# Two linear-attention and feed-forward layers on one core: banks by age, statistics from accumulating ops, a reordered attention phase

## The chip, the cores and the metric

The kernel runs on one core of a Trainium2 chip. The metric is device time in microseconds of one execution; a run's time is given as the median of several. The engines are PE (TensorE), DVE (VectorE), ACT (ScalarE), POOL (GpSimd) and SP (SyncE, which here only issues DMAs).

## The reference, cut to what matters

```python
def _A_ref(x, wqkv, wo):             # H = 32 heads of 16, D = 512, S = 2048
    q, k, v = qkv[0], qkv[1], qkv[2]
    phi = lambda t: jnp.where(t > 0, t + 1, jnp.exp(t)) + 1e-6
    pq, pk = phi(q), phi(k)
    kv = jnp.einsum("bhsd,bhse->bhde", pk, v)
    z = jnp.einsum("bhsd->bhd", pk)
    num = jnp.einsum("bhqd,bhde->bhqe", pq, kv)
    den = jnp.einsum("bhqd,bhd->bhq", pq, z)[..., None] + 1e-6
    return (num / den).transpose(...).reshape(B, S, D) @ wo
def _B_ref(x, w_gate, w_up, w_down):  # F = 1792
    return (_silu(x @ w_gate) * (x @ w_up)) @ w_down
x = x + _A_ref(_layernorm(x), A_wqkv, A_wo)
x = x + _B_ref(_layernorm(x), B_w_gate, B_w_up, B_w_down)
x = x + _A_ref(_layernorm(x), A_wqkv, A_wo)
x = x + _B_ref(_layernorm(x), B_w_gate, B_w_up, B_w_down)
```

## The kernel before

All weights and the activations X stay in SBUF. The 2048 tokens are 16 tiles of 128, or four groups of 512 (four tiles each). Layers are numbered 0 to 3: 0 and 2 are attention, 1 and 3 feed-forward.

**Layer norm** (`ln`, L402). For one tile, DVE takes statistics (L408, L409), POOL makes variance plus epsilon and its power -0.5 (L410, L413), and ACT applies them (L426, after one more POOL operation, L422) or, for the first four tiles, DVE (L430). The normalised tile is then transposed into xnT: by a DMA transpose that SP issues (L445), or, for the first four tiles, by PE with a copy by DVE (L438, L442).

**Attention.** `k_proj` makes a tile's k in four matmuls; `phi` (L452) turns it into pk by an exponential on ACT (L454), a minimum on DVE (L456) and a DVE operation that reads the bank again (L459). `g_acc` accumulates G = xn^T pk over all 16 tiles in banks 0 to 3, `z_acc` the sum of pk. `g_copy`, `kvt`, `m_mm` make from G the matrix Mo that takes the place of v, kv and wo. `q_proj` makes a chunk (128 features) of a group's q, with phi. `den` (L536) multiplies q by z in 16 small matmuls, takes the reciprocal on DVE, spreads it on ACT (L553), has it transposed by four DMAs from SP (L557) and multiplies it into the four chunks of q on DVE (L562), each over the whole group. `wo` (L566) multiplies a tile by Mo, adds into X on DVE (L573) and starts the next layer's `ln`.

**Feed-forward.** `gu` makes one of 14 chunks of gate and up for a group, with a tanh on ACT and two DVE operations; `dn` multiplies a tile by w_down, adds into X (L611) and starts the next `ln`.

**Order.** PE's order is the order in which the code calls these functions, written out by hand (L660 to L720); `weave` mixes a list of fill blocks into a feed-forward group. The other queues are ordered by `schedule` (L58): it places each instruction by costs given in the code (`occ`, `lat`), takes what can start earliest on an engine, and breaks ties by a due time worked back from PE's order. Every queue then runs in that fixed order on the chip and waits on semaphores. X's seven loads (L372 to L379) are such ties; their `lat` is 2.3 for tile 0, 3.0 + 0.5t for tiles 1 to 3. PSUM has eight banks: gate and up take 0 to 3 in turn, k and q banks 4 and 5, the rest 6 and 7. The weights are 15 DMAs from POOL of 256 to 512 KB: two at once, then one after each key tile of layer 0, at most four in flight.

In layer 0 the key phase runs k_proj of all 16 tiles with g_acc two tiles behind. Then come z, g_copy, kvt, m_mm, q of groups 0 to 2 with their den, and wo of groups 0 and 1; gate and up of layer 1 start, with the rest of q, den and wo as fill. In layer 2 the key tiles 0 to 11 are fill of layer 1's groups, and g_acc follows.

Of the kernel before, what the change touches and what calls it, by code (L numbers as in the profile page):

```python
# [11 lines left out]
SEM = 0.06  # L12


class Op:
    __slots__ = ("i", "eng", "fn", "deps", "occ", "lat", "dma", "lane", "start", "end", "need", "val",
                 "dead", "succ", "pos", "tag")


class Prog:  # L20
# [5 lines left out]
    def __init__(self, lanes):  # L26
        self.ops = []
        self.bufs = {}
        self.lanes = lanes

    def op(self, eng, fn, r=(), w=(), occ=0.5, lat=None, after=(), dma=False, tag=""):
        o = Op()
        o.i = len(self.ops)
        o.eng, o.fn, o.occ, o.dma, o.tag = eng, fn, occ, dma, tag
        o.lat = lat if lat is not None else occ + 0.09
        o.need = dma
# [18 lines left out]
        self.ops.append(o)  # L55
        return o

    def schedule(self):  # L58
# [4 lines left out]
        t = 0.0  # L63
        pe_time = {}
        for o in ops:
            if o.eng == "pe":
                pe_time[o.i] = t
                t += o.occ
        for o in reversed(ops):
            dead = t + 50.0  # L70
            for s in o.succ:
                s = ops[s]
                dead = min(dead, s.dead - o.lat - SEM)
            if o.eng == "pe":
                dead = min(dead, pe_time[o.i])
            o.dead = dead
        nd = {o.i: len(o.deps) for o in ops}
        free = {e: 0.0 for e in self.ENGINES}
# [4 lines left out]
        xbar = 0.0  # L83
# [21 lines left out]
        while left:  # L105
            best = None
            for e in self.ENGINES:
# [7 lines left out]
                cand = None  # L115
                for o in avail[e]:
                    s = max(free[e], rt_of[o.i])
                    key = (s, o.dead, o.i)
                    if cand is None or key < cand[0]:
                        cand = (key, o)  # L120
                if cand is not None and (best is None or cand[0][0] < best[0]):
                    best = (cand[0][0], cand[1])
# [4 lines left out]
            if o.dma == "t":  # L127
                xbar = max(xbar, s + 0.6) + 1.0
                o.end = xbar + 1.2
            else:  # L130
                o.end = s + o.lat
# [123 lines left out]
def bass_interleave_layers__linear_attn_block__swiglu_ffn__prompt_kernel(  # L255
# [20 lines left out]
    with stack:  # L276
# [9 lines left out]
        negh = sb("negh", [P, 1], FP32)  # L286
        Wqkv = sb("Wqkv", [P, NC, 3 * D], BF16)
# [14 lines left out]
        nmr = sb("nmr", [P, T], FP32)  # L302
        NE = 4
        etmp = [sb("etmp", [P, 512], BF16) for _ in range(NE)]
        pk = [sb("pk", [P, D], BF16) for _ in range(T)]
        NPQ = 12
        pq = [sb("pq", [P, 512], BF16) for _ in range(NPQ)]
        GT = sb("GT", [P, NC, D], BF16)
        KVT = sb("KVT", [P, NC, P], BF16)
        Mo = sb("Mo", [P, NC, D], BF16)  # L310
# [13 lines left out]
        r_gu = Ring([0, 1, 2, 3])  # L324
        r_kq = Ring([4, 5])
        r_tok = Ring([6, 7])
# [9 lines left out]
        r_ost = Ring(range(8, NPQ))  # L336
# [13 lines left out]
        op("pool", lambda g: g.memset(negh[:], -0.5), w=["negh"], occ=0.1)  # L350
        op("pool", lambda g: g.memset(ident[:], 0.0), w=["ident"], occ=0.2)
# [4 lines left out]
        def late_consts(after):  # L356
            mask3 = mask[:].rearrange("p (h j) -> p h j", j=DH)
            op("pool", lambda g: g.memset(ones[:], 1.0), w=["ones"], occ=0.1, after=after)
# [276 lines left out]
        for t in range(TG, T):  # L635
            ln(0, t)
# [118 lines left out]
```

## Time and profile before

| | us |
|---|---|
| median of 3 runs | 476.61 (474.79 to 477.08) |
| the profiled execution, its own time | 478.77 |
| its span, first to last instruction | 477.0 |
| PE busy in the span | 435.2 (91%) |
| DVE busy | 327.8 (69%) |
| ACT busy | 171.6 (36%) |
| POOL busy | 77.2 (16%) |
| mean granted clock of PE | 0.964 of 2.4 GHz |

Busy shares are means over stages that differ, so the span has to be cut before they say anything. Matmul records overlap by design: 0.38 us of one matmul's record is not its cost, the start-to-start distance is.

### The profile page before, as it was taken

The page shows a single profiled execution, that of the slowest core. Times are in us where ns is not written, and L with a number is a line of the kernel's source. Part 1 is how long each engine was busy: PE and PEld are TensorE (multiplying, and loading weights), DVE is VectorE, ACT ScalarE, POOL GpSimd, SP SyncE. Part 2 cuts the span into 40 slices and gives each one's busy share as a digit, 9 for nine tenths or more (in the row PEclk, how much of TensorE's full clock was granted, in tenths as well). Part 3 has the DMA queues.
Part 4 walks back from the last instruction along what each step waited for, and adds up shares of the span by engine and source line. Part 5 has one row for each costly group of instructions (what it writes and reads, how often), then busy time and mean ns, then how long its engine had stood idle before and what let it go on. Part 6 is the DMA issues. An engine that isn't in the chain of part 4 may idle for free.

```text
span 477.0 us, 6447 instructions
## 1 busy us (share of the span) xinstructions
PE 435.2 (91%) x2182; PEld 194.2 (41%) x2182; DVE 327.8 (69%) x613; ACT 171.6 (36%) x277; POOL 77.2 (16%) x214
## 2 busy tenths in 40 slices
PE   4788967899999999999999996678999999999997
PEld 1333522244444444444444342223444444444443
DVE  3964679599679858867873267959856873763761
ACT  0672452645334414324322135263532331321320
POOL 3871103311122020012003000331100110000000
PEclk9799977799999999999999997999999999999999
DMA  8399522421221111001001002242221012001001
GB/s 276 82 230 159 202 56 45 88 43 37 44 45 23 24 22 23 0 9 38 0 1 34 11 2 56 45 80 48 41 45 43 12 22 57 1 2 44 1 0 44
DMA packets 56656, 24.27 MB, mean 51 GB/s; under 512 B 50672, under 2 KB 55280, under 8 KB 56624
## 3 DMA queue, kind: packets, MB, share of 16 engines
q1 hardware_dynamic: 54512, 16.27, 16.1%
q0 software_dynamic: 1584, 7.08, 5.6%
q10 hardware_dynamic: 528, 0.52, 0.4%
q8 instruction: 17, 0.28, 0.2%
q14 instruction: 15, 0.12, 0.1%
HBM read 9.70 MB, written 2.10 MB: 25 GB/s over the span
## 4 chain that ended last, share of the span: by engine, by line
PE 73%; DVE 9%; DMA 7%; SPq 5%; POOL 2%; issue 2%; ACT 2%; DVEq 0%; ACTq 0%; POOLq 0%
PE pb L343 72%; DMA xnT<-xnA 3%; SPq L557 3%; DMA RT<-rrep 2%; SPq L445 2%; DVE stats L408 2%; DVE pq L459 2%; DVE X L573 1%; DMA X<-in_A_x_dram 1%; POOL rstd L413 1%; DVE pq L562 1%; ACT etmp L454 1%; DVE etmp L456 1%; POOL vpe L410 1%; DVE Mo L500 1%
## 5 line engine op out<-in xcount | busy, mean ns | idle before, releaser
L343 PE MATMUL pb<-xnT,Wg 128*128 128x512 bf16 x448 | 115.8, 381 | 5.5 <-DMA xnT<-xnB 5.3
L343 PE MATMUL pb<-xnT,Wu 128*128 128x512 bf16 x448 | 115.9, 381 | 1.4 <-DVE hT L596 1.4
L591 ACT ACTIVATE tht<-pb 128x512 f32<-128x512 f32 x112 | 66.5, 595 | 124.5 <-PE pb L343 112.9
L343 PE MATMUL pb<-Wd,hT 128*128 128x512 bf16 x448 | 98.0, 379 | 0.0
L593 DVE SCALAR_TENSOR_TENSOR tht<-tht,pb 128x512 f32<-128x512 f32 x112 | 76.5, 683 | 26.3 <-ACT tht L591 25.7
L596 DVE TENSOR_TENSOR hT<-tht,pb 128x512 bf16<-128x512 f32 x112 | 76.8, 686 | 9.8 <-DVE mv L409 0.4
L343 PEld LDWEIGHTS pb<-xnT,Wg 128*128 128x128 bf16 x448 | 43.8, 98 | 59.6 <-issue 7.4
L343 PEld LDWEIGHTS pb<-xnT,Wu 128*128 128x128 bf16 x448 | 44.0, 98 | 55.2 <-DVE hT L596 2.1
L343 PEld LDWEIGHTS pb<-Wd,hT 128*128 128x128 bf16 x448 | 43.7, 98 | 52.4
L410 POOL TENSOR_SCALAR vpe<-mv 128x1 f32<-128x1 f32 x64 | 14.6, 236 | 288.6 <-DVE mv L409 287.4
L454 ACT ACTIVATE etmp<-pb 128x512 bf16<-128x512 f32 x64 | 37.9, 594 | 64.4 <-PE pb L343 57.5
L408 DVE BATCH_NORM_STATS2 stats<-X 128x6 f32<-128x512 bf16 x64 | 42.8, 682 | 7.4 <-DMA X<-in_A_x_dram 6.6
L456 DVE TENSOR_SCALAR etmp<-etmp 128x512 bf16<-128x512 bf16 x64 | 18.8, 294 | 36.0 <-ACT etmp L454 34.5
L343 PE MATMUL pb<-Mo,pq 128*128 128x512 bf16 x128 | 36.1, 419 | 6.0 <-DVE pq L562 4.5
L343 PE MATMUL pb<-xnT,Wqkv 128*128 128x512 bf16 x128 | 36.9, 421 | 4.9 <-DVE pq L459 3.4
L343 PE MATMUL pb<-Wqkv,xnT 128*128 128x512 bf16 x128 | 34.0, 390 | 5.6 <-DMA xnT<-xnA 2.1
L426 ACT ACTIVATE xnB<-X,nmr,rstd 128x512 bf16<-128x512 bf16 x32 | 25.3, 809 | 36.8 <-POOL nmr L422 30.6
L426 ACT ACTIVATE xnA<-X,nmr,rstd 128x512 bf16<-128x512 bf16 x28 | 22.7, 812 | 42.9 <-POOL nmr L422 42.9
L413 POOL TENSOR_TENSOR rstd<-vpe,negh 128x1 f32<-128x1 f32 x64 | 36.2, 570 | 5.5 <-POOL vpe L410 0.5
L343 PE MATMUL pb<-pk,xnA 128*128 128x512 bf16 x128 | 31.1, 379 | 0.0
L611 DVE SCALAR_TENSOR_TENSOR pq<-pb,X 128x512 bf16<-128x512 f32 x16 | 11.1, 691 | 28.9 <-PE pb L343 28.9
L459 DVE SCALAR_TENSOR_TENSOR pk<-pb,etmp 128x512 bf16<-128x512 f32 x32 | 22.1, 690 | 2.7
(51 smaller groups left out, 231.5 us busy)
## 6 DMA issues: line engine op xcount, KB each, us to landing
out_dram<-pq SPq DMA_DIRECT2D x16, 128.0 KB, 1.7
Wg<-in_B_w_gate_dram POOLq DMA_DIRECT2D x4, 448.0 KB, 7.5
Wu<-in_B_w_up_dram POOLq DMA_DIRECT2D x4, 448.0 KB, 10.7
X<-in_A_x_dram SPq DMA_DIRECT2D x3, 512.0 KB, 9.2
Wd<-in_B_w_down_dram POOLq DMA_DIRECT2D x3, 512.0 KB, 6.6
Wqkv<-in_A_wqkv_dram POOLq DMA_DIRECT2D x2, 512.0 KB, 6.8
Wqkv<-in_A_wqkv_dram ACTq DMA_DIRECT2D x1, 512.0 KB, 4.4
X<-in_A_x_dram SPq DMA_DIRECT2D x4, 128.0 KB, 4.4
```

The costliest lines, as they stand in the source:

```text
L343: return op("pe", lambda e: e.matmul(o_ap, lhsT=lhsT, rhs=rhs, start=start, stop=stop, skip_group_check=skip), r=r, w=w, occ=occ, lat=occ ...
L408: op("dve", lambda v: v.bn_stats(stats[:, t, :], X[:, t, :]), r=[xk], w=[f"st{t}"], occ=0.6)
L410: op("pool", lambda p: p.tensor_scalar(out=vpe[:, t:t + 1], in0=mv[:, t, 1:2], scalar1=1e-5, scalar2=None, op0=ALU.add), r=[f"mv{t}"], w=[ ...
L413: op("pool", lambda p: p.tensor_tensor(out=rstd[:, t:t + 1], in0=vpe[:, t:t + 1], in1=negh[:], op=ALU.pow), r=[f"vp{t}", "negh"], w=[f"rs{ ...
L426: op("act", lambda a: a.activation(out=b_ap, in_=X[:, t, :], func=ACT.Identity, bias=nmr[:, t:t + 1], scale=rstd[:, t:t + 1]), r=[xk, f"nm ...
L454: op("act", lambda a: a.activation(out=etmp[e][:], in_=PB[pb][:], func=ACT.Exp), r=[f"pb{pb}"], w=[f"e{e}"], occ=0.485, lat=0.6)
L456: op("dve", lambda v: v.tensor_scalar(out=etmp[e][:], in0=etmp[e][:], scalar1=1.0, scalar2=1e-6, op0=ALU.min, op1=ALU.add), r=[f"e{e}"], w ...
L459: op("dve", lambda v: v.scalar_tensor_tensor(out=dst, in0=PB[pb][:], scalar=0.0, in1=etmp[e][:], op0=ALU.max, op1=ALU.add), r=[f"pb{pb}", ...
L557: op("sp", lambda e, tl=tl, q=q: e.dma_start(RT[R][:, :, tl * P:(tl + 1) * P], rrep[q][:], transpose=True), r=[f"rrep{q}"], w=[f"RT{R}_{tl ...
L591: op("act", lambda e: e.activation(out=tht[a][:], in_=PB[pg][:], func=ACT.Tanh, scale=0.5), r=[f"pb{pg}"], w=[f"th{a}"], occ=0.485, lat=0.6)
L593: op("dve", lambda v: v.scalar_tensor_tensor(out=tht[a][:], in0=tht[a][:], scalar=1.0, in1=PB[pg][:], op0=ALU.add, op1=ALU.mult), r=[f"pb{ ...
L596: op("dve", lambda v: v.tensor_tensor(out=hT[h][:, j, :], in0=tht[a][:], in1=PB[pu][:], op=ALU.mult), r=[f"pb{pu}", f"th{a}"], w=[f"h{h}_{ ...
```

## The change

- **Planner.** Ties on a queue go by due time among all instructions that can start within 0.1 us (`HOLD`); DMAs are modelled by two pipes with a transfer time each; a DMA may carry a fixed priority. X's loads and the key weights get one, in tile order; the key weights are two DMAs instead of one, the larger X loads 256 KB instead of 512.
- **PSUM.** Banks are given by age: the one whose last use lies furthest back; the four banks of G and the one of z are pinned while they accumulate.
- **Layer norm.** In layers 1 to 3 the sum of X comes from the adding operation itself (`accum_out` in wo and dn), and the sum of squares from a Square on ACT; one small DVE operation makes the negative mean. The apply is on DVE, in layer 0 from tile 4 on wherever planned load is lighter. The first four tiles' transposes are copied out by ACT.
- **phi.** Two forms, chosen by planned load: as before, or with the add on ACT (a second activation from the bank) and a maximum on DVE from SBUF.
- **q and den.** A group's q is one tile, and the multiply by the reciprocal goes by token tile, each after its own transpose. Mo is written over G.
- **Order.** The key phase takes z along, and in layer 0 eight q products (groups 0 and 1). q of group 3 moves from the feed-forward fill ahead of it. The weights start after key tile 7, two per tile.

```diff
-            o.dead = dead
+            o.dead = dead if o.prio is None else o.prio
...
+                at = {o.i: max(free[e], rt_of[o.i]) for o in avail[e]}
+                lim = min(at.values()) + HOLD
+                o = min((o for o in avail[e] if at[o.i] <= lim), key=lambda o: (o.dead, o.i))
...
-        r_gu = Ring([0, 1, 2, 3])
-        r_kq = Ring([4, 5])
-        r_tok = Ring([6, 7])
+        def bank(pin=False):
+
+            def last(b):
+                st = pr.bufs.get(f"pb{b}")
+                return max([st[0]] + st[1] + [stamp[b]]) if st else stamp[b]
+            b = min((b for b in range(8) if b not in pinned), key=lambda b: (last(b), b))
...
+        for t in range(TG):
+            dma("sp", X[:, t, :], x2d[t * P:(t + 1) * P, :], 128, w=[f"x{t}"], prio=-100 + t)
+        dma("act", Wqkv[:, 0:2, D:2 * D], wq3[:, 0:2, D:2 * D], 256, w=["Wk0"], prio=-100)
+        dma("act", Wqkv[:, 2:4, D:2 * D], wq3[:, 2:4, D:2 * D], 256, w=["Wk1"], prio=-99)
...
+                op("dve", lambda v: v.tensor_scalar(out=mv[:, t, 0:1], in0=sums[:, t:t + 1], scalar1=-1.0 / D,
+                                                    scalar2=None, op0=ALU.mult),
+                   r=[f"sm{t}"], w=[f"mv{t}"], occ=0.07, lat=0.14)
+                op("act", lambda a: a.activation(out=b_ap, in_=X[:, t, :], func=ACT.Square,
+                                                 bias=mv[:, t, 0:1], accum_out=mv[:, t, 1:2]),
+                   r=[xk, f"mv{t}"], w=[bk, f"ss{t}"], occ=0.62, lat=0.75)
...
-                op("dve", lambda v: v.tensor_copy(out=dst, in_=tp[:, 0:512].rearrange("p (c k) -> p c k", c=NC)),
-                   r=[f"pb{pb}"], w=[f"xt{sl}_{tl}"], occ=0.4)
+                op("act", lambda a: a.activation(out=dst, in_=src, func=ACT.Copy),
+                   r=[f"pb{pb}"], w=[f"xt{sl}_{tl}"], occ=0.664, lat=0.77)
...
+            if mode == "act":
+                op("act", lambda a: a.activation(out=dst, in_=PB[pb][:], func=ACT.Identity, bias=onep[:]),
+                   r=[f"pb{pb}", "onep"], w=dk, occ=0.485, lat=0.6)
...
+            if mode == "act":
+                op("dve", lambda v: v.tensor_tensor(out=dst, in0=dst, in1=etmp[e][:], op=ALU.max),
+                   r=[f"e{e}"] + dk, w=dk, occ=0.335, lat=0.42)
...
+                op("dve", lambda v, ap=ap, tl=tl: v.tensor_tensor(out=ap, in0=ap,
+                                                                  in1=RT[R][:, :, tl * P:(tl + 1) * P], op=ALU.mult),
+                   r=ks + [f"RT{R}_{tl}"], w=ks, occ=0.335, lat=0.42)
...
-            op("dve", lambda v: v.tensor_tensor(out=X[:, t, :], in0=PB[pb][:], in1=X[:, t, :], op=ALU.add),
-               r=[f"pb{pb}", f"x{t}"], w=[f"x{t}"], occ=0.607, lat=0.69)
+            op("dve", lambda v: v.scalar_tensor_tensor(out=X[:, t, :], in0=PB[pb][:], scalar=1.0, in1=X[:, t, :],
+                                                       op0=ALU.mult, op1=ALU.add, accum_out=sums[:, t:t + 1]),
...
-        for i in range(14):
+        spin(11)
+        ln(0, 0, pe_t=True)
+        spin(2)
...
         for t in range(T):
+            if t < TG - 1:
+                ln(0, t + 1, pe_t=True)
             k_proj(0, t)
...
+            if t >= 7:
+                load_next(2)
             if t >= LAG:
-                g_acc(t - LAG)
+                gz(0, t - LAG)
+            if t >= 10:
+                q(0, *divmod(t - 10, NC))
+        q(0, 1, 2)
+        gz(0, T - 2)
+        q(0, 1, 3)
+        gz(0, T - 1)
...
         for L in (0, 2):
+            z_fin(L)
+            g_copy()
+            if L == 2:
+                q(L, 0, 2, 3)
+                q(L, 1, 0, 1, 2, 3)
+            else:
+                q(L, 2, 0)
+            den(L, 0)
             kvt()
+            q(L, 2, 1)
             m_mm()
+            q(L, 2, 2)
             den(L, 1)
+            q(L, 2, 3)
+            wos(L, 0)
+            q(L, 3, 0)
+            wos(L, 1, [0, 1])
+            q(L, 3, 1)
+            wos(L, 1, [2, 3])
+            q(L, 3, 2, 3)
             den(L, 2)
```

## Rows read from the trace of the kernel before

**Rows 1.** Stages: length, busy PE, PEld, DVE, ACT, POOL; clock, DMA share, GB/s.

```profile
15.30:52.00 36.70, 32.18 (x143) 13.05 (x142) 23.47 (x56) 19.73 (x32) 19.48 (x48) 0.97 0.83 186
52.00:89.30 37.30, 26.86 (x205) 11.72 (x202) 29.50 (x66) 16.98 (x30) 5.88 (x16) 0.82 0.28 65
89.30:257.50 168.20, 167.96 (x784) 75.93 (x785) 127.44 (x223) 64.98 (x102) 26.92 (x77) 0.99 0.14 27
257.50:279.60 22.10, 21.04 (x151) 9.85 (x150) 6.67 (x14) 5.26 (x9) 1.32 (x4) 1.00 0.09 17
279.60:316.00 36.40, 24.36 (x146) 10.01 (x145) 29.34 (x66) 17.42 (x31) 5.89 (x18) 0.86 0.23 45
316.00:477.00 161.00, 156.17 (x736) 70.52 (x736) 104.05 (x170) 46.35 (x76) 10.88 (x31) 1.00 0.13 30
```

**Rows 2.** Timeline, 0 to 61 us: start, duration, engine, line, operation, [idle before].

```profile
0.80 3.47 SPq L369 DMA_DIRECT2D X<-in_A_x_dram  x7
...
7.82 0.69 DVE L408 BATCH_NORM_STATS2 stats<-X 128x6 f32<-128x512 bf16 x1 [6.63 <-DMA X<-in_A_x_dram]
...
11.15 0.59 PE L438 MATMUL pb<-ident,xnA 128*128 128x128 bf16 x4 [5.27 <-POOL vpe L410]
...
14.44 1.28 ACT L426 ACT_TABLE_LOAD   x1 [14.44 <-POOL nmr L422]
...
15.29 3.17 PE L343 MATMUL pb<-Wqkv,xnT 128*128 128x512 bf16 x8
...
59.60 0.55 PE L343 MATMUL pb<-Zm,pq 128*128 128x8 bf16 x16
```

**Rows 3.** The chain that ended last, in order of time: start, duration, what.

```profile
2.18 5.62 DMA X<-in_A_x_dram
...
63.25 1.19 SPq L557
64.53 1.22 SPq L557
...
67.16 2.45 DMA RT<-rrep
...
138.41 130.54 PE pb L343 x604
```

**Rows 4.** Waits of PE: engine, line, releaser: us in total, times, longest.

```profile
PE pb L343 <- DVE pq L459: 10.7, 13, 2.6
PE pb L343 <- DMA xnT<-xnB: 5.3, 2, 3.0
```

**Rows 5.** DMA issues (first X load; POOL's Wqkv; transposes from 32 to 34 us): median us to landing.

```profile
X<-in_A_x_dram SPq DMA_DIRECT2D x1, 128.0 KB, 2.2
...
Wqkv<-in_A_wqkv_dram POOLq DMA_DIRECT2D x2, 512.0 KB, 6.8
...
xnT<-xnA SPq DMA_TRANSPOSE x2, 13.2
```

**Rows 6.** Groups by line and shape: busy us, mean ns | idle before it.

```profile
L408 DVE BATCH_NORM_STATS2 stats<-X 128x6 f32<-128x512 bf16 x64 | 42.8, 682 | 7.4 <-DMA X<-in_A_x_dram 6.6
...
L454 ACT ACTIVATE etmp<-pb 128x512 bf16<-128x512 f32 x64 | 37.9, 594 | 64.4 <-PE pb L343 57.5 <-DVE pk L459 4.5 <-DVE pq L459 1.1
...
L459 DVE SCALAR_TENSOR_TENSOR pk<-pb,etmp 128x512 bf16<-128x512 f32 x32 | 22.1, 690 | 2.7
...
L456 DVE TENSOR_SCALAR etmp<-etmp 128x512 bf16<-128x512 bf16 x64 | 18.8, 294 | 36.0 <-ACT etmp L454 34.5
...
L562 DVE TENSOR_TENSOR pq<-pq,RT 128x512 bf16<-128x512 bf16 x32 | 12.1, 418 | 5.8 <-DMA RT<-rrep 5.8
...
L409 DVE BATCH_NORM_AGGREGATE mv<-stats 128x2 f32<-128x6 f32 x64 | 10.0, 171 | 1.8
...
L430 DVE TENSOR_SCALAR xnA<-X,mv,rstd 128x512 bf16<-128x512 bf16 x4 | 1.6, 402 | 0.2 <-POOL rstd L413 0.2
```

**Rows 7.** Windows: the 17th microsecond, columns as in Rows 1.

```profile
16.00:17.00 1.00, 1.00 (x4) 0.30 (x3) 1.00 (x3) 0.55 (x1) 0.82 (x4) 0.50 0.00 0
```

More of the change, by code (lines that the diff above doesn't have):

```diff
@@ L29, in __init__, with lighter, after, op @@
         self.lanes = lanes
-    def op(self, eng, fn, r=(), w=(), occ=0.5, lat=None, after=(), dma=False, tag=""):
+        self.clock = {e: 0.0 for e in self.ENGINES}
+    def lighter(self, **loads):
+        def after(name):
+            c = dict(self.clock)
+            for e, x in loads[name].items():
+                c[e] = max(c[e], c["pe"]) + x
+            return max(c["act"], c["dve"]), sum(loads[name].values())
+        return min(loads, key=after)
+    def op(self, eng, fn, r=(), w=(), occ=0.5, lat=None, after=(), dma=0.0, prio=None):
         o = Op()
         o.i = len(self.ops)
-        o.eng, o.fn, o.occ, o.dma, o.tag = eng, fn, occ, dma, tag
+        o.eng, o.fn, o.occ, o.dma, o.prio = eng, fn, occ, dma, prio
         o.lat = lat if lat is not None else occ + 0.09
-        o.need = dma
+        o.need = dma > 0
         o.succ = []
@@ L55, in op @@
         self.ops.append(o)
+        c = self.clock
+        c[eng] = (c[eng] if eng == "pe" else max(c[eng], c["pe"])) + occ
         return o
@@ L62, in schedule @@
                 ops[d].succ.append(o.i)
[L63 to L68, printed above, removed]
+        t = sum(o.occ for o in ops if o.eng == "pe")
+        after = t
         for o in reversed(ops):
@@ L74, in schedule @@
             if o.eng == "pe":
-                dead = min(dead, pe_time[o.i])
-            o.dead = dead
+                dead = after = min(dead, after - o.occ)
+            o.dead = dead if o.prio is None else o.prio
         nd = {o.i: len(o.deps) for o in ops}
-        free = {e: 0.0 for e in self.ENGINES}
+        free = {e: 0.6 for e in self.ENGINES}
+        free["act"] = 0.61
         avail = {e: [] for e in self.ENGINES}
@@ L114, in schedule @@
                     continue
[L115 to L122, printed above, removed]
+                if not avail[e]:
+                    continue
+                at = {o.i: max(free[e], rt_of[o.i]) for o in avail[e]}
+                lim = min(at.values()) + HOLD
+                o = min((o for o in avail[e] if at[o.i] <= lim), key=lambda o: (o.dead, o.i))
+                if best is None or at[o.i] < best[0]:
+                    best = (at[o.i], o)
             assert best is not None, "stuck"
@@ L126, in schedule @@
             free[o.eng] = s + o.occ
-            if o.dma == "t":
-                xbar = max(xbar, s + 0.6) + 1.0
-                o.end = xbar + 1.2
+            if o.dma:
+                k = o.lat > 2.5
+                pipe[k] = max(pipe[k], s + o.occ + 0.9) + o.dma
+                o.end = pipe[k] + 0.6
             else:
@@ L480, in z_acc @@
             if L not in zb:
-                zb[L] = r_tok.take()
+                zb[L] = bank(pin=True)
             pb = zb[L]
@@ L504, in g_copy @@
             for c in range(NC):
-                evac(c, GT[:, c, :], f"GT{c}", "act" if c % 2 == 0 else "dve")
+                evac(gb[c], GT[:, c, :], f"GT{c}")
+                pinned.discard(gb[c])
         def kvt():
-            pb = r_tok.take()
+            pb = bank()
             for c in range(NC):
@@ L527, in q_proj @@
             sl = slot_of[L, g]
-            pb = r_kq.take()
+            pb = bank()
             for c in range(NC):
@@ L584, in gu @@
             sl = slot_of[L, g]
-            pg, pu = r_gu.take(), r_gu.take()
+            pg, pu = bank(), bank()
             for pb, W, wk in ((pg, Wg, "Wg"), (pu, Wu, "Wu")):
@@ L601, in dn @@
             h = hb[L, g]
-            pb = r_tok.take()
+            pb = bank()
             for j in range(NF):
```

270 lines of the change are left out of this document (136 added, 134 removed).

## The prediction

> **What bounds the kernel now.** I first cut the span into its stages at matmul landmarks [rows 1]: key phase of layer 0 (K1), its attention part (A1), its feed-forward part (B1), and the same for layer 2 (K2, A2, B2), with the start ahead of them. In B1 TensorE is busy 167.96 of 168.20 us and in B2 156.17 of 161.00, so nothing off TensorE is worth anything there. The loss sits in the start, where the first key matmul comes at 15.29 [rows 2], and in A1 and A2, where TensorE is busy 26.86 of 37.30 and 24.36 of 36.40 us. Its granted clock averages 0.82 and 0.86 of 2.4 GHz there, so part of the busy time is at the lower level, 1.2 GHz.
>
> To see how much of a stage is work I price a 512-column matmul at full clock: 604 of them in 130.54 us [rows 3], 0.216 us each, 0.86 for the four of a product. A1 holds 40 for q, 32 for wo and 4 for Mo: 16.4 us. Its 128 small ones (64 for z, 48 for den, 16 for KVT) go at 0.034, as 16 for den take 0.55 [rows 2]: 4.4. So 20.8 of 37.3 us is work and 16.5 is lost. A2 has no z to speak of: 18.6 is work and 17.8 lost.
>
> Next, which wait ends last: TensorE waits for phi's vector instruction to free a bank (10.7 us in 13 waits) and for transposes of the normalised tiles (5.3 us) [rows 4]. The chain shows where the latter come from [rows 3]: den, reciprocal, broadcast, then transposes that SyncE issues one by one, 1.28 us apart, the last landing 2.45 us after its issue ends. VectorE is busy 29.50 of A1's 37.30 us [rows 1].
>
> **Start.** The first statistic runs at 7.82 after a wait of 6.63 us, though the first 128 KB transfer, issued at 0.80, landed within 2.2 [rows 2, 5]. The fourth ended at 2.18 plus 5.62, which is 7.80 [rows 3], so it is tile 0 that came fourth: the old planner sorts loads by due time, and the longer assumed landing of tile 3 makes it due first. The change pins the order, and two weight loads of 512 KB no longer share the queues: tile 0 lands near 3.0. From there I keep today's sequence, 7.82 to 11.15 from statistic to first transpose [rows 2], less a second statistic in between (0.68): 5.7. Four transposes take 0.6. The copy out moves to ScalarE and is its first activation, so the table load of 1.28 us, now off the path, stands in it; then 0.6 for the copy, like ScalarE's exponential from PSUM (0.594) [rows 2, 6], and I put 0.4 for hand-overs. First key matmul: **8.6** (7.3 without the table load; 12.0 if tile 0 still takes 5.6).
>
> **K1.** It now holds 16 key, 16 g and 8 q products: 160 matmuls, 34.6 us, and z, 2.2. Losses: at the lower clock [rows 7] eight matmuls took 3.17 us [rows 2], 0.18 each too much; ten cost 2 us (none, if the dummies hold the clock). Banks: key and q share three instead of two, since five are pinned; I put 1.2 us for waits on phi. Weights: Wq is issued after the phi of key tile 7, near 24.3 (8.6, seven key and five g products with z, the clock, then a product and phi), takes 6.8 [rows 5] and lands near 31; TensorE reaches the first q at 29: 2.0 us (0 to 4). The last transposes of this stage take 13.2 us today, beside four weight loads [rows 5]; issued by 29 they would land by 42, and key tile 15 is due near 44: nothing, with 4 as the bad end. K1 is **42.1**, to 50.7.
>
> **A1 and A2.** TensorE needs 68 matmuls (8 q products, 8 wo, Mo), KVT and three den in A1: 16.9 us. A2 has 13 q products, 21.2: the list of layer 2 never issues chunk 0 of group 2 of q, so den and wo use what layer 0 left there, 0.86 less. SyncE's chain: den starts 0.9 after the last g, the first reciprocal transpose 3.65 later (59.60 to 63.25 [rows 2, 3]), then four for group 0, four for group 1 and four for normalised tiles before gate/up may start. That is 12 at 1.3 and 2.45 to land: **22.6**. In A2 six q products stand ahead of den: 26.9. That wo 0 now follows the first transpose instead of the fourth is what lets this chain run without a pause.
>
> VectorE must fit too. Of its 29.5 us in A1, statistics go (8 at 0.682 and 0.171, 6.8), two phi leave (0.98 each) and half of the other eight take 0.71 (0.294 and 0.418) instead, 1.1 less; there come the apply, 8 at 0.402, and the mean, 8 at 0.171 as the nearest small operation: 4.6 [rows 6]. That leaves **24.2**, more than SyncE's chain, and I take it. A2 by the same steps, with three phi more and half of 13 in the new form: **28.2**. ScalarE, busy 17 us of 37, covers the Square, which I price like its 0.594 activation [rows 6]; without that cover four of them stand in the chain, 2.4 us. Whether the sum that the accumulating add also writes costs VectorE anything no row shows: from nothing, since the pass is the same (and a gain is excluded, since the add stays), to another 0.171 each, 1.4 per stage. I take nothing and keep 2.8 for the range.
>
> The Trainium skill speaks against part of this: ScalarE: Activation LUTs, Rules for kernel authors, wants max, min, add and mul on VectorE, up to about three times as fast in bf16. Here the source is PSUM, and the rows differ: phi's add from PSUM takes 0.690 on VectorE, an activation from PSUM 0.594 on ScalarE [rows 6]. By the rule the second form would gain nothing, and the sum would be 2.9 us higher. The measurement decides.
>
> **B1, K2, B2.** Four q products leave the first feed-forward group, where TensorE was full: 3.5 us each, no gain by itself, since A1 and A2 now carry them. B1 is 164.7. K2 idles 1.1 us today; half is taken: 21.6. B2 idles 4.8, mostly the end of the run; 0.7 is taken: 156.8. Cheaper statistics save VectorE time here, but TensorE does not wait for it: zero. The weights are in by then: some 6.9 MB from 24 us at K1's 186 GB/s [rows 1] end near 62, and gate/up starts at 75.
>
> **Sum.** 8.6 + 42.1 + 24.2 + 164.7 + 21.6 + 28.2 + 156.8 = 446.2 us against 477.0: 30.8 less. The profiled execution took 478.77 (1.8 around its span), 2.2 over the median of 476.61; taken off the median that is **445.8**.
>
> **Rivals.** (1) TensorE bounds both attention stages: 16.9 and 21.2, 14.3 less, **431.5**. For it: eight banks, and gate/up does not need the vector work of tiles 4 to 7. Against: SyncE's chain alone is longer. 0.15. (2) The attention stages lose what they lose now, because queues are in order and one late vector instruction holds phi behind it: 33.4 and 39.0, 20.0 more, **465.8**; half of it, 455.8. For it: VectorE near full. Against: four times the free banks. 0.13. (3) Later weights meet A1's reciprocal transposes: one flight takes 13.2 instead of 2.4, 10.8 more, **456.6**. For it: weights run to 62 and A1 starts at 50.7. Against: only half of the stage. 0.12. (4) Slower: Square is not in the activation table that is loaded. The profile shows one load, 1.28 us [rows 2], that serves Exp, Tanh, Copy and Identity; no Square runs. Each of 48 Squares would cost two loads, 2.57 us: eight in each attention stage, ahead of broadcasts and exponentials on ScalarE, and four in K2, 51 us, **497**. It is slower than before once 12 of the 48 stand in the path. 0.03. (5) The forecast, 0.57.
>
> Beside (4): the Trainium skill (ScalarE: Activation LUTs, Table sets) has the cheap functions in every set, without this one among its examples.
>
> The forecast's own bounds (start 1.3 less or 3.4 more, K1 4 either way, accumulation 2.8), rivals 1 and 3 and half of 2 give 430 to 460; beyond it lie the worse half of 2, and 4. Half a per cent is about what a measurement here tells from no change. All cases but (4) are faster by more; I keep 0.02 for a meeting of 2 and 3 that ends level and one point more for slower.
>
> **What would show it.** First key matmul near 9; the table load just ahead of ScalarE's first copy; a wait for Wq of some 2 us in K1; A1 and A2 near 24 and 28 us, granted clock above 0.9, VectorE over 90% busy, transposes 1.3 apart without pause; B1 and B2 as full as now. Wrong would be: a first statistic later than 5, table loads at every Square, A1 over 30, idle TensorE in B1.

## The result and the profile after

The changed kernel's median is **444.9 us** (443.4 to 446.8, four runs) against 475.7 us for the kernel before, run beside it: a ratio of 0.935, 95% interval 0.930 to 0.940. The profiled execution took 443.97 us with a span of 442.2. Faster was forecast, 445.8 us in 430 to 460. Ratios leave out runs more than 1.5% above the fastest run of their kernel; of the changed kernel and its variants that takes out two of the four runs of experiment 6.

First the span cut at the same landmarks as [rows 1], with the start as a stage of its own. Columns: stretch, length, busy PE, PEld, DVE, ACT, POOL; granted clock, DMA share, GB/s.

```profile
0.00:7.67 7.67, 5.42 (x21) 2.02 (x22) 3.62 (x10) 1.88 (x2) 2.52 (x14) 1.00 0.76 247
7.67:48.40 40.73, 36.82 (x231) 17.55 (x233) 29.79 (x75) 26.71 (x45) 25.25 (x58) 1.00 0.78 214
48.40:72.70 24.30, 17.88 (x134) 8.41 (x136) 20.61 (x64) 18.64 (x38) 3.27 (x8) 1.00 0.44 96
72.70:237.10 164.40, 163.56 (x753) 74.44 (x769) 114.61 (x244) 71.16 (x141) 19.88 (x54) 0.99 0.14 28
237.10:257.70 20.60, 20.42 (x150) 10.14 (x152) 6.83 (x16) 4.49 (x9) 1.20 (x3) 1.00 0.07 14
257.70:286.50 28.80, 23.25 (x155) 10.77 (x155) 25.18 (x75) 22.19 (x45) 3.77 (x9) 0.94 0.31 56
286.50:442.20 155.70, 151.72 (x705) 69.22 (x720) 100.31 (x174) 44.81 (x86) 8.85 (x23) 1.00 0.13 31
```

| stage | before | forecast | after |
|---|---|---|---|
| start | 15.3 | 8.6 | 7.7 |
| K1 | 36.7 | 42.1 | 40.7 |
| A1 | 37.3 | 24.2 | 24.3 |
| B1 | 168.2 | 164.7 | 164.4 |
| K2 | 22.1 | 21.6 | 20.6 |
| A2 | 36.4 | 28.2 | 28.8 |
| B2 | 161.0 | 156.8 | 155.7 |
| span | 477.0 | 446.2 | 442.2 |

Of the 34.8 us that the span lost, 20.6 come from A1 and A2, 9.1 from B1 and B2, 7.6 from the start and 1.5 from K2; K1 gives 4.0 back for six q products more (it held two before) and z. Some of this is work that changed its stage: those six products (5.2 us at the prediction's 0.86) and z (2.2) left A1, and four q products (3.5) left each of B1 and B2 for A1 and A2, so 7.0 of the 9.1 us are moved and not saved. Counted with the prediction's prices, the time that is not work falls from 16.5 to 7.4 us in A1 and from 17.8 to 7.6 in A2. The changed kernel also leaves out one q product of layer 2, 0.86 us of work that the kernel before does; experiment 9 has it back.

The waits of TensorE after (us in total, times, longest) answer to [rows 4]. L366 is every matmul of the program, L514 phi's old add, L626 the multiply by the reciprocal:

```profile
PE pb L366 <- DMA xnT<-xnB: 5.6, 2, 3.3
PE pb L366 <- DVE pq L626: 4.6, 6, 2.6
PE pb L366 <- DMA Wqkv<-in_A_wqkv_dram: 2.6, 1, 2.6
...
PE pb L366 <- DVE pq L514: 0.6, 1, 0.6
```

Of the 10.7 us of waits for phi's old add, 0.6 are left. Not all of them were waits for a bank. In the kernel before, four of the thirteen, 6.3 us, stand ahead of den's small products, which read what phi has just written; two of them, the others being equal in A2:

```profile
63.51 0.26 PE L343 MATMUL pb<-Zm,pq 128*128 128x8 bf16 x4 [0.51 <-DVE pq L459]
...
66.39 0.27 PE L343 MATMUL pb<-Zm,pq 128*128 128x8 bf16 x4 [2.62 <-DVE pq L459]
```

Only the other nine, 4.4 us, stand ahead of products that need nothing from phi but its bank. The order, which now puts other products between a group's q and its den, took the first kind away, and the banks the second (experiment 2).

The wait for the normalised tiles' transposes ahead of gate and up has stayed (5.3 before), and there is a new one for Wq. The timeline of the same kernel, start, duration, engine, line, [idle before]; L445 is the statistic, L620 and L489 are SyncE's transposes of reciprocals and of normalised tiles, L452 the means:

```profile
1.80 1.28 ACT L486 ACT_TABLE_LOAD   x1 [1.80 <-issue]
3.38 0.69 DVE L445 BATCH_NORM_STATS2 stats<-X 128x6 f32<-128x512 bf16 x1 [2.19 <-DMA X<-in_A_x_dram]
7.67 1.03 PE L366 MATMUL pb<-Wqkv,xnT 128*128 128x512 bf16 x4
30.45 1.02 PE L366 MATMUL pb<-xnT,Wqkv 128*128 128x512 bf16 x4 [2.57 <-DMA Wqkv<-in_A_wqkv_dram]
52.28 11.51 SPq L620 DMA_TRANSPOSE RT<-rrep  x8
63.89 7.48 SPq L489 DMA_TRANSPOSE xnT<-xnB  x4
64.45 0.43 DVE L626 TENSOR_TENSOR pq<-pq,RT 128x512 bf16<-128x512 bf16 x1 [1.76 <-DMA RT<-rrep]
64.79 0.27 DVE L452 TENSOR_SCALAR mv<-sums 128x1 f32<-128x1 f32 x3
72.73 1.41 PE L366 MATMUL pb<-xnT,Wg 128*128 128x512 bf16 x4 [3.32 <-DMA xnT<-xnB]
```

The first statistic runs at 3.38 instead of 7.82 [rows 2]. A1 is bounded by a chain that changes engines: SyncE's eight reciprocal transposes, the landing of one, VectorE's means and applies, SyncE again. The chain of waits from 60 to 73 us shows the hand-over:

```profile
60.11 4.32 DMA RT<-rrep
...
64.45 0.43 DVE pq L626
64.88 0.18 DVE mv L452 x3
...
69.02 0.33 DVE xnB L473
...
70.15 2.44 DMA xnT<-xnB
```

The planner fixes the order of VectorE's queue. The multiply at 64.45 waits 1.76 us for its transpose, and behind it stand three means whose sums were ready: three tiles' normalisation waits for a transpose that it doesn't need. Last, the groups: line, engine, operation, count | busy us, mean ns:

```profile
L452 DVE TENSOR_SCALAR mv<-sums 128x1 f32<-128x1 f32 x48 | 6.6, 149 | 0.8
L455 ACT ACTIVATION_READ_ACCUMULATOR xnB<-X,mv 128x1 f32 x32 | 6.2, 192 | 0.0
L637 DVE DVE_READ_ACCUMULATOR X<-pb,X 128x1 f32 x32 | 2.6, 83 | 0.0
```

An operation that also sums is two instructions: the pass, and a read of the accumulator, 83 ns on VectorE and 192 ns on ScalarE (there behind a Square of 721 ns on tiles of the feed-forward layers).

### The profile page after: what moved, and what is told of

The parts are those of the page before. It is cut to its first block, busy times and chain, and to the rows that moved or that the text cites. A ratio compares the mean times of both kernels' runs of the same rounds, so it can differ in the third digit from the quotient of the medians.

```text
span 442.2 us, 6441 instructions
## 1 busy us (share of the span) xinstructions
PE 419.1 (95%) x2135; PEld 192.6 (44%) x2177; DVE 301.0 (68%) x653; ACT 189.9 (43%) x361; POOL 64.7 (15%) x167
## 4 chain that ended last, share of the span: by engine, by line
PE 81%; DVE 7%; DMA 4%; POOL 3%; ACT 2%; issue 2%; SPq 1%; DVEq 0%; ACTq 0%
PE pb L366 81%; POOL rstd L462 2%; DVE X L637 1%; DMA Wqkv<-in_A_wqkv_dram 1%; SPq L620 1%; DMA xnT<-xnB 1%; DMA RT<-rrep 1%; DVE stats L445 1%; DVE pq L514 1%; DMA X<-in_A_x_dram 1%; ACT rrep L616 1%; DVE etmp L507 1%; POOL vpe L447 1%; DVE xnB L473 1%; POOL nmr L466 0%
## 5 line engine op out<-in xcount | busy, mean ns | idle before, releaser
L366 PE MATMUL pb<-xnT,Wg 128*128 128x512 bf16 x439 | 114.9, 381 | 6.1 <-DMA xnT<-xnB 5.6
L366 PE MATMUL pb<-xnT,Wu 128*128 128x512 bf16 x438 | 114.4, 381 | 0.5
L366 PE MATMUL pb<-Wd,hT 128*128 128x512 bf16 x438 | 97.1, 379 | 0.6
L366 PEld LDWEIGHTS pb<-xnT,Wg 128*128 128x128 bf16 x448 | 43.9, 98 | 58.8 <-issue 6.8
L366 PEld LDWEIGHTS pb<-xnT,Wu 128*128 128x128 bf16 x448 | 44.1, 98 | 53.5 <-issue 1.1
L366 PEld LDWEIGHTS pb<-Wd,hT 128*128 128x128 bf16 x448 | 43.7, 98 | 52.4
L458 POOL TENSOR_SCALAR vpe<-mv 128x1 f32<-128x1 f32 x48 | 10.0, 208 | 267.6 <-ACT xnB L455 159.1
L366 PE MATMUL pb<-GT,pq 128*128 128x512 bf16 x127 | 33.3, 394 | 5.2 <-DVE pq L626 4.6
L366 PE MATMUL pb<-xnT,Wqkv 128*128 128x512 bf16 x118 | 29.7, 378 | 2.9 <-DMA Wqkv<-in_A_wqkv_dram 2.6
L366 PE MATMUL pb<-Wqkv,xnT 128*128 128x512 bf16 x123 | 32.1, 378 | 0.3
L366 PE MATMUL pb<-pk,xnA 128*128 128x512 bf16 x127 | 32.2, 378 | 0.1
L455 ACT ACTIVATE xnB<-X,mv 128x512 bf16<-128x512 bf16 x32 | 23.0, 721 | 13.0 <-DVE mv L452 11.6
L473 DVE TENSOR_SCALAR xnA<-X,mv,rstd 128x512 bf16<-128x512 bf16 x20 | 8.2, 411 | 26.4 <-POOL rstd L462 26.3
L455 ACT ACTIVATE xnA<-X,mv 128x512 bf16<-128x512 bf16 x16 | 11.5, 722 | 33.7 <-DVE mv L452 33.7
L637 DVE SCALAR_TENSOR_TENSOR X<-pb,X 128x512 bf16<-128x512 f32 x32 | 21.9, 684 | 2.0 <-PE pb L366 2.0
```

The lines of the kernel that those rows point to most:

```text
L366: return op("pe", lambda e: e.matmul(o_ap, lhsT=lhsT, rhs=rhs, start=start, stop=stop, skip_group_check=skip), r=r, w=w, occ=occ, lat=occ ...
L455: op("act", lambda a: a.activation(out=b_ap, in_=X[:, t, :], func=ACT.Square, bias=mv[:, t, 0:1], accum_out=mv[:, t, 1:2]), r=[xk, f"mv{t} ...
L458: op("pool", lambda p: p.tensor_scalar(out=vpe[:, t:t + 1], in0=mv[:, t, 1:2], scalar1=1.0 / D, scalar2=1e-5, op0=ALU.mult, op1=ALU.add), ...
L473: op("dve", lambda v: v.tensor_scalar(out=b_ap, in0=X[:, t, :], scalar1=mean, scalar2=rstd[:, t:t + 1], op0=sub, op1=ALU.mult), r=[xk, f"m ...
L637: op("dve", lambda v: v.scalar_tensor_tensor(out=X[:, t, :], in0=PB[pb][:], scalar=1.0, in1=X[:, t, :], op0=ALU.mult, op1=ALU.add, accum_o ...
```

## The experiments

Each run below is a whole kernel, timed against the kernel before on the same chip. The comparison is of ratios: the changed kernel's is 0.935 (0.930 to 0.940), and 0.01 is 4.8 us. Differences under about 3 us between two variants are not resolved. Stage lengths are those of one profiled execution each, and they scatter too: K1, the same in the changed kernel and in experiments 8 (b) and (c), took 40.6, 42.5 and 42.2 us there, with a granted clock of 1.00, 0.71 and 0.57 in the 4 us around 32.

**1. The banks as before** (rings of four, two and two; all else as changed).

```diff
...
-            b = min((b for b in range(8) if b not in pinned), key=lambda b: (last(b), b))
...
+        r_gu = Ring([0, 1, 2, 3])
+        r_kq = Ring([4, 5])
+        r_tok = Ring([6, 7])
...
```

> The banks go back to fixed rings (four for gate and up, two for k and q, two for the rest); all else as changed. Theory 'banks carry the gain': TensorE waits again for phi to free a bank, about the 10.7 us of the kernel before, spread over both attention parts and the key phase, and the time is near 456. Rival 'the chain from den to gate/up sets these parts, the banks only let TensorE run ahead': less than 3 us slower, below 448.

Measured: 455.99 us, ratio 0.959 (0.955 to 0.962), 11 us slower than the changed kernel. K1 took 43.1 us, A1 26.9, A2 32.0. Waits of TensorE, L505 being phi's add here, and the timeline's first gate/up product:

```profile
PE pb L357 <- DMA xnT<-xnB: 9.7, 2, 4.8
PE pb L357 <- DVE pq L505: 3.4, 6, 1.0
```

```profile
77.33 1.87 PE L357 MATMUL pb<-xnT,Wg 128*128 128x512 bf16 x4 [4.85 <-DMA xnT<-xnB]
```

The price is the one expected, but only a part of it bears the expected name. The waits for phi come back with 3.4 us, all ahead of q products: nearly the 4.4 us of the kernel before that were waits for a bank. Two early key products wait another 1.3 and 1.1 us for phi. More is a longer wait for the transposes (9.7 us instead of 5.6); why they come later with the rings was not followed up. The first four gate/up matmuls after the 4.85 us wait take 1.87 us, against 1.03 at 2.4 GHz: the granted clock is 0.50, which is 1.2 GHz, in the next 4 us, and B1 is 1.7 and B2 2.9 us longer.

**2. Statistics as before** in all layers, no accumulating ops.

```diff
-            if L == 0:
+            if True:
...
-            op("dve", lambda v: v.scalar_tensor_tensor(out=X[:, t, :], in0=PB[pb][:], scalar=1.0, in1=X[:, t, :],
-                                                       op0=ALU.mult, op1=ALU.add, accum_out=sums[:, t:t + 1]),
+            op("dve", lambda v: v.tensor_tensor(out=X[:, t, :], in0=PB[pb][:], in1=X[:, t, :], op=ALU.add),
```

> Statistics of layers 1 to 3 by bn_stats and bn_aggr on VectorE again, no accumulating add, no Square, no mean; the apply stays on VectorE. Theory 'VectorE's amount of work sets both attention parts' (the prediction): 8 times 0.85 less 0.15 come back in each, 5.4 to 5.6 us, so near 456. Rival 'order': VectorE is busy only 85 to 87 per cent there, the statistics are as long a piece of the chain as mean, Square and their accumulator read (0.85 against 1.1 us), and the time stays within 2 us of 444.9.

Measured: 452.23 us, ratio 0.953 (0.949 to 0.957): 7 to 8 us slower. A1 is 25.9 (+1.5), A2 30.8 (+1.9), B2 158.7, and the wait for the transposes 8.5 us in two (longest 5.3) instead of 5.6. By VectorE's amount of work each stage should have grown by 5.0 us (eight tiles, each 0.853 for the two statistics of [rows 6] instead of 0.149 for the mean and 0.083 for the accumulator read); it grew by less than half of that. B2's 3.0 us more go with a granted clock of 0.52 and 0.62 in the eight microseconds around its first gate/up product, so part of the price is paid behind the wait. Another 1.8 us of this profile's 7.5 stand in K1, which the edit leaves alone.

**3. phi in one form**, the old one.

```diff
-            return pr.lighter(dve=dict(act=0.485, dve=0.81), act=dict(act=1.06, dve=0.54))
+            return "dve"
```

> phi only in the form whose add VectorE does out of PSUM. Theory 'VectorE's amount of work': 1.1 us more in the first attention part, 1.8 in the second, and the key phase, where VectorE is busy 29.8 of 40.7, is not bound: near 448. Rival 'order': the second form on ScalarE queues ahead of the Squares of the normalisation there, so taking it away gives back what VectorE pays: within 1 us of 444.9 or faster.

Measured: 443.46 us, ratio 0.931 (0.926 to 0.936): no loss, inside the interval. A1 is 24.8 us, A2 28.5. Moving phi's add to ScalarE gained nothing that can be measured, although by [rows 6] it takes 0.3 us per chunk from VectorE. The Trainium skill (ScalarE: Activation LUTs, Rules for kernel authors) wants adds and maxima on VectorE. This run is in line with that: the form that keeps the add there is no slower, 443.46 us against 444.9.

**4. The weights at once**, as before: Wq and Wv first, then one per key tile.

```diff
-        wi = [0]
+        wi = [2]
+        weights[0]([])
+        weights[1]([])
...
-            if t >= 7:
-                load_next(2)
+            load_next(1)
```

> The later weights alone are undone: Wq and Wv are issued at once and one of the rest after every key tile, as in the kernel before; all else as changed. Theory (the weights' order sets the key phase): the first transposes land beside 1.5 MB of weights as they did before, so the first key product starts 1 to 2 us later than the 7.67 us of the changed kernel; the last transposes land some 13 us after their issue, and TensorE waits for them in the key phase, now that the bank waits are gone that hid it: the key phase is 3 to 6 us longer, 449 to 453 us in all. Rival (hidden anyway): the transposes are issued early enough, and Wq there from the start saves the 2.57 us wait for it: 443 to 446 us.

Measured: 450.80 us, ratio 0.949 (0.945 to 0.953): 6 us slower, the theory's size. It is all in K1, 47.4 us. The theory's first step, a later start, failed: the first key product comes at 7.28, no later than in the changed kernel. TensorE's waits, and X's larger loads with their median time to landing (5.2 us in the changed kernel):

```profile
PE pb L481 <- DVE xnA L473: 4.0, 2, 3.3
PE pb L366 <- DMA xnT<-xnA: 3.9, 3, 1.7
PE pb L366 <- ACT xnA L469: 1.5, 1, 1.5
```

```profile
X<-in_A_x_dram SPq DMA_DIRECT2D x6, 256.0 KB, 8.3
```

The larger X loads land 3 us later and the transposes of layer 0's tiles are waited for: K1 pays both, the start neither.

**5. Wq earlier**: (a) Wq after key tile 4, the rest as changed; (b) the same, with the rest three per tile from key tile 10.

```diff
+            if t == 4:
+                load_next(1)
```

```diff
-            if t >= 7:
-                load_next(2)
+            if t == 4:
+                load_next(1)
+            if t >= 10:
+                load_next(3)
```

> The changed kernel with Wq issued after key tile 4 instead of 7; the other weights as changed. Theory: the 2.6 us that TensorE waits for Wq in the key phase of layer 0 are all on the path, since the key phase is TensorE's: 2.6 us less, near 442.3. Rival: POOL is busy 9 of 10 us between 10 and 20 us with the normalisation, a DMA issue of 0.9 us there holds the later tiles' transposes, and the wait only changes its name: within 1 us of 444.9 or slower.

> Wq alone is issued after key tile 4, and the rest three per tile from key tile 10 on, all else as changed. Theory (only one load stands beside the transposes): neither the 2.57 us wait for Wq is left nor the 3.3 us wait for the last transposes that came in its place when Wq was moved ahead of an otherwise unchanged order; the key phase falls by 2 to 3 us, 442 to 443 us. Rival: the last weights are then still landing when the first stage between key phase and gate/up needs its reciprocal transposes, which took 4.3 us instead of 2.4 beside weights already: that stage grows by as much, 444 to 447 us; or one load alone is enough to delay the transposes, and the wait of 3 us for xnT stays.

Measured: (a) 446.13 us, ratio 0.939 (0.936 to 0.942), no gain; (b) 448.37 us, 0.943 (0.940 to 0.947), some 4 us slower. Waits in (a), then in (b), then in (b) the timeline's first multiply by the reciprocal that has to wait in A1:

```profile
PE pb L366 <- DMA xnT<-xnA: 3.3, 1, 3.3
```

```profile
PE pb L366 <- DMA xnT<-xnA: 4.2, 1, 4.2
```

```profile
62.90 0.42 DVE L626 TENSOR_TENSOR pq<-pq,RT 128x512 bf16<-128x512 bf16 x1 [3.16 <-DMA RT<-rrep]
```

The wait for Wq is gone in both, and one for a transpose has its place. It is the transpose of key tile 9, in the middle of the phase. Its chain in (a), then in (b):

```profile
19.39 7.68 DMA xnT<-xnA
```

```profile
19.24 8.64 DMA xnT<-xnA
```

SyncE issued it at the same moment as GpSimd issued Wq's load (19.37 and 19.21), and it landed after 7.68 and 8.64 us, where the transposes issued before 19 us landed in 2.5. In (b) no other weight load is issued before 35.22, so a single 512 KB load beside them is enough. In (b) the late weights also meet A1's reciprocal transposes (3.16 us of wait instead of 1.76), which is rival 3.

Where does Wq's lateness come from? The changed kernel's chain of waits:

```profile
14.10 1.25 POOL rstd L462 x2
...
24.80 0.52 POOL rstd L462
25.32 4.99 DMA Wqkv<-in_A_wqkv_dram
```

From 13.7 to 25.3 the chain stays on GpSimd, almost without a gap: the normalisation of layer 0's tiles, its power operations above all, stands ahead of the load in the queue that issues it. The load was to follow the phi of key tile 7, which ended at 23.6, so the queue held it for 1.7 us. It is not the landing that makes Wq late: 4.99 us is less than the 6.8 of [rows 5].

**6. q of groups 0 and 1 back** in the attention stage of layer 0.

```diff
-            if t >= 10:
-                q(0, *divmod(t - 10, NC))
...
+                q(L, 0, 0, 1, 2, 3)
+                q(L, 1, 0, 1, 2, 3)
```

> Layer 0 is ordered like layer 2: the eight q products of groups 0 and 1 stand after the key phase, ahead of den. Key phase and attention part of layer 0 take 40.7 and 24.3 us in the changed kernel. Theory 'TensorE bounds the key phase': it sheds eight products (6.9) and the wait for Wq (2.6), to 31.2, and the attention part grows by the 6.9 to 31.2, so the sum of the two falls from 65.0 to about 62.4 and the run is some 2.6 us faster than the changed kernel, near 442. Rival 'q fills waits in the key phase, that is what the move is for': the key phase stays above 37, the sum is above 68, and the run is 4 us or more slower, above 448.

Measured: 441.40 and 443.65 us in the two runs that the ratio rests on, 0.931 (0.926 to 0.936), no loss; the other two took 448.25 and 452.01. The profiled run is the one of 448.25, so only its waits are read:

```profile
PE pb L366 <- DMA xnT<-xnA: 4.4, 1, 4.4
```

Without q the key phase waits 4.4 us for one of its last transposes; q had filled that, and waits for Wq instead. That moving q into the key phase gains anything by itself is not shown, and two runs decide little.

**7. X's loads in tile order, alone**, in the kernel before: the fixed priorities of the first four loads and nothing else.

```diff
+        for t in range(TG):
+            dma("sp", X[:, t, :], x2d[t * P:(t + 1) * P, :], 128, w=[f"x{t}"], prio=-100 + t)
```

> The kernel before with nothing but X's loads issued in tile order. Theory: the first statistic starts near 3.3 instead of 7.8, the first key product 4.5 us earlier than 15.3, and the time falls by about 4.5, to 471. Rival 'the key phase is bound by its last transposes, which wait behind the weights': they land when they land, and the gain is under 2 us.

Measured: 475.94 us, ratio 1.000 (0.997 to 1.004). The timeline:

```profile
3.00 0.69 DVE L409 BATCH_NORM_STATS2 stats<-X 128x6 f32<-128x512 bf16 x1 [1.82 <-DMA X<-in_A_x_dram]
...
9.00 0.59 PE L439 MATMUL pb<-ident,xnA 128*128 128x128 bf16 x4 [2.76 <-POOL vpe L411]
12.37 1.03 PE L439 MATMUL pb<-ident,xnA 128*128 128x128 bf16 x8 [2.79 <-DVE xnA L431]
...
14.66 3.62 PE L344 MATMUL pb<-Wqkv,xnT 128*128 128x512 bf16 x8
```

The first statistic moves from 7.82 to 3.00, and the first key product only from 15.29 to 14.66: the old order has the transposes of all four tiles ahead of it. So the loads alone don't give the start's gain. The changed kernel has the transposes between the key products as well; that step was not tried by itself.

**8. Order of A1 alone.** In none of the three kernels is an instruction added or removed. (a) was meant to take group 0's normalisation first, by a fixed due time; that due time was handed back to all that stands ahead of it, and the means ran last instead. In (b) it counts only where the planner chooses. (c) takes the first den of layer 2 ahead of group 1's q.

```diff
-                   r=[f"sm{t}"], w=[f"mv{t}"], occ=0.07, lat=0.14)
+                   r=[f"sm{t}"], w=[f"mv{t}"], occ=0.07, lat=0.14, prio=first)
...
```

```diff
+        for o in ops:
+            if o.early:
+                o.dead = -1000.0
...
```

```diff
                 q(L, 0, 2, 3)
+                den(L, 0)
+                q(L, 1, 0, 1)
+                kvt()
-                q(L, 1, 0, 1, 2, 3)
+                q(L, 1, 2, 3)
...
```

> In the planner the normalisation of group 0 in layers 1 and 3 (mean, Square, variance, power, apply) goes ahead of anything else that can start. No instruction is added or removed. Theory 'order': the waits of 3.3 and 2.3 us for the transposes ahead of gate/up, and part of the lower clock behind them, shrink, since means of tiles 1 to 3 no longer stand behind a multiply that waits for its reciprocal: 3 to 5 us less, 440 to 442. Rival 'VectorE's amount of work': the same work in another order, something else comes late, within 1 us of 444.9.

> In layers 1 and 3 the mean, the Square, the variance, the power and the apply of group 0's four normalisations are taken ahead of whatever else is ready on their engines; nothing is added or removed. Theory (order): in the changed kernel the means of tiles 1 to 3 stand on VectorE behind a phi multiply that waits 1.76 us for its transpose, in each of the two stages between the last key-sum product and the first gate/up products; with each mean right behind its add the wait of TensorE for the transposes ahead of the first gate/up products falls from 3.32 us to 1.5 or less, and the two stages lose 1.5 to 2.5 us each: 440 to 442 us. Rival (amount of VectorE's work): it has the same work in the stage, so what goes first only moves the wait to the phi products behind: 444 to 446 us, with the wait for VectorE's pq grown by what the transposes' wait lost.

> In layer 2 den of group 0 moves ahead of the four q products of group 1. Theory 'the chain from den to gate/up sets this part': it starts 3.5 us earlier while TensorE's work (21.2 us) still fits, so the part falls from 28.8 to near 25.4 and the run is 3.4 us faster, near 441.5. Rival 'amount of work': VectorE's 25.2 busy us of 28.8 stay, the part ends within 1 us of now.

Measured: (a) 457.47 us, ratio 0.961 (0.957 to 0.966), 12 us slower, A1 35.8. (b) 442.38 us, 0.930 (0.927 to 0.933), A1 23.1 (24.4), A2 unchanged at 28.9. (c) 443.22 us, 0.932 (0.928 to 0.936), A2 28.0 instead of the 25.5 that 3.4 us less would make. The means and the first gate/up product in (a):

```profile
70.41 0.51 DVE L453 TENSOR_SCALAR mv<-sums 128x1 f32<-128x1 f32 x7
...
85.93 1.87 PE L366 MATMUL pb<-xnT,Wg 128*128 128x512 bf16 x4 [14.93 <-DMA xnT<-xnB]
```

and the latter in (b):

```profile
72.97 1.02 PE L370 MATMUL pb<-xnT,Wg 128*128 128x512 bf16 x4 [1.93 <-DMA xnT<-xnB]
```

(a) failed as an experiment on its theory, but it shows the size of order: the same instructions in another order cost A1 11.4 us. In (b) the wait falls from 3.32 to 1.93 us, 1.3 of the 1.5 to 2.5 us expected in A1 and nothing in A2. B1 is shorter as well, 162.7 us instead of 164.4: the granted clock in the 4 us behind that product is 1.00 where it was 0.57. The median's 2.5 us are at the edge of what is resolved.

**9. Together**, (b) and (c) of the last, q's first product of the key phase one key tile later, and the product that the changed kernel leaves out issued.

```diff
...
-            if t >= 10:
-                q(0, *divmod(t - 10, NC))
+            if t >= 11:
+                q(0, *divmod(t - 11, NC))
+        q(0, 1, 1)
...
+                q(L, 2, 0)
```

> Three things together: group 0's means and what follows them first (as in the run of the means first), the first denominator of layer 2 ahead of group 1's q (as in its own run), and new: q's first product of layer 1's phase one key tile later, after tile 11 instead of 10, the one left over issued behind the loop. Layer 2's chunk 0 of group 2 of q, which the changed kernel leaves out, is issued: 0.86 us more for TensorE. Theory (the wait for Wq costs itself and the lower clock behind it): Wq lands at about 30.4 us, the product then starts at about 29.9, so the wait falls from 2.57 us to 1 or less, the clock stays 1.00 in the 8 us behind it (it was 0.71 and 0.57 for 4 us in two of the profiles with waits of 2.8 us), and the key phase takes 38 to 40 us; with the means first -2.5, the denominator -1, the extra product +0.9: 438 to 441 us. Rival (the wait is only moved: TensorE then waits for the last transposes, which land beside the weights, or for group 1's phi, which come later now, in the next stage): 442 to 445 us.

Measured: **440.22 us** (439.0 to 441.4), ratio 0.925 (0.920 to 0.929), clear of the changed kernel's interval. It is not clear of (b) alone, so what each of the other parts adds is read from the stages: K1 is 38.7 us, below the 40.6 to 42.5 of the profiles that wait for Wq, and no wait for Wq or the last transposes is left in it; A1 is 23.0, A2 28.9 with a product more. Windows of 4 us behind the place of that wait, columns as above, first in this kernel, then in the run of the means first, which waits 2.8 us for Wq:

```profile
30.00:34.00 4.00, 3.87 (x22) 1.88 (x23) 2.67 (x6) 1.25 (x3) 1.85 (x3) 1.00 1.20 262
```

```profile
30.00:34.00 4.00, 3.68 (x12) 1.47 (x13) 1.53 (x4) 1.19 (x2) 1.86 (x3) 0.71 1.14 297
```

## Why the prediction was right, step by step

The value and the range held. The stages came out within 1.4 us each, and the sum is 4.0 high in the span, with every difference but two (A1 0.1, A2 0.6) on the same side. That the median came within 0.9 us is luck in part: I took 2.2 us off because the profiled run before was slower than its median, and the profiled run after is 0.9 faster than its own.

**Start, 8.6 against 7.67.** The cause of the late statistic was right: tile 0 landed fourth, and pinned it lands near 3. Two steps failed. "The table load of 1.28 us, now off the path, stands in it": it runs at 1.80, ahead of any data, and costs nothing. It is the only one in the changed kernel's trace. And weights that no longer share the queues are not what helps tile 0: with them at once the first key product comes at 7.28. The order of loads alone didn't give the gain either (experiment 7).

**K1, 42.1 against 40.7.** Neither the lower clock (2) nor bank waits (1.2) were seen in the profile of the changed kernel; the 2.0 for Wq were 2.57, put together from other sizes: issued at 25.3 and not 24.3, for GpSimd's queue, landed in 4.99 and not 6.8, and wanted at 27.9 and not 29. For the last transposes I took nothing, and that held because q's products stand ahead of them: without q they cost 4.4 us (experiment 6), and with q a key tile later and no wait for Wq still nothing (experiment 9). What the later weights are worth, 6 us, I had not counted as a term: I took it from the 13.2 us of [rows 5] that the transposes would land in time, which is the same mechanism without its price.

**A1 and A2, 24.2 and 28.2 against 24.3 and 28.8.** The sizes were right and the reason was half wrong. I took VectorE's amount of work as the bound and said over 90% busy; it was busy 20.61 of 24.30 and 25.18 of 28.80 us, 85% and 87%, so the amount itself came out 3.6 and 3.0 us under my sums. The bound is the chain through SyncE and VectorE's queue. SyncE's part by itself, 22.6, was nearest in form, but it does pause: eight transposes in 11.51 and four in 7.48 us, 19.0 instead of 15.6. Its sum also counts an issue too many: the 2.45 us to landing run from the start of the last issue and not from its end (70.15 plus 2.44 above), which makes it 21.3. The amount did not set the length: 5.0 us more of it in a stage cost 1.5 and 1.9 us (experiment 2), and the same amount in another order takes 23.1 us (experiment 8 b) or 35.8 (8 a). That nearly the forecast time came out is, in this part, a coincidence of two sums that lay close together. The reading of [rows 4] that stood ahead of the stages was half wrong too: 6.3 of its 10.7 us were den waiting for phi's result and not for a bank.

**Accumulation, nothing against 0.083 each**, inside the bounds; 0.7 us for the eight of a stage. The Trainium skill (VectorE: DVE Perf Modes, Two Vector instructions with no wait between them) has an op with an accumulator as two instructions; the trace shows both. The Square is 0.721 plus 0.192, not 0.594.

**phi's second form.** I took 0.294 and 0.418 on VectorE for 0.98 and so 2.9 us in two stages; the form gains nothing (experiment 3). The step failed with its premise: VectorE's time was not what was short.

**The rivals.** Rival 2 (queues in order hold the stages up) names the right mechanism; its size is seen where the order is bad (experiment 8 a). Rival 3 exists in small: one transpose landed in 4.32 instead of 2.45 us, and experiment 5 (b) raised it. Rival 4 is refuted: the one table load serves Square too. Rival 1 stays some 6 us away in each stage, TensorE being busy 17.88 of 24.30 and 23.25 of 28.80.

**B1, B2, K2.** 164.4 and 155.7 against 164.7 and 156.8; in K2 the one wait for a bank, 1.04 us ahead of a key product in the trace before, is gone whole where I took half of the idle time; the rest of the 1.0 was not looked into. The undone parts cost 11 us (banks), 7 (statistics), 6 (weights), and nothing that can be measured for phi's form and q's place. They need not add up, since several act on the same wait.

## What to carry to other kernels

When a stage is bounded by a chain through several in-order queues, look first at what stands ahead of the ready instruction on each engine: here a mean of 0.15 us behind a multiply that waited, and a weight load behind GpSimd's small operations. A wait that an edit removes can be only the first of two that end close together, so look for the next one before you price it (Wq and the transposes). Price a large load beside small transposes by undoing it: 6 us here, all in the key phase and none of it in the start, where I had looked for some of it. Before you call a wait one for a bank, look at what the waiting instruction reads.

## What was not expected of the hardware

After a wait TensorE may run at the lower of its levels (1.2 GHz, a granted clock of 0.50) for some microseconds, so the wait costs more than itself. Granted clock in the 4 us behind the first gate/up product of layer 1, in the changed kernel (wait 3.32 us ahead), then in the run with the old banks (4.85 us):

```profile
72.73:76.73 4.00, 4.00 (x11) 1.50 (x12) 1.68 (x6) 3.25 (x8) 0.94 (x3) 0.57 0.43 86
```

```profile
77.33:81.33 4.00, 4.00 (x10) 1.43 (x11) 2.22 (x5) 1.65 (x5) 1.49 (x4) 0.50 0.60 103
```

The length of the last wait doesn't settle it: behind 1.93 us the clock was 1.00 in the run of the means first and 0.62 in the combined one, and behind the 2.57 us for Wq it was 1.00 in the changed kernel, 0.71 behind 2.83 us in the run of the means first and 0.57 behind 2.46 us in the run of the early den. What decides was not tried.
